# The second MoE layer takes its tokens in one chunk of 256 and four chunks of 512

## The chip, the cores and the metric

The kernel runs on one core of a Trainium2 chip. The metric is the device time of one execution in microseconds (us), as the median of several runs. Durations inside an execution come from one profiled execution, in which the engines are named PE (TensorE matmul), PEld (its weight load), DVE (VectorE), ACT (ScalarE), POOL (GpSimd) and SP (the engine that issues the transfers).

## What is computed

Attention with a decay mask makes 2304 token rows of 512 values. Two feed-forward layers (here "layer 1" and "layer 2", each 512 to 2048 to 512) follow:

```python
x = np.ascontiguousarray(attn_out.transpose(0, 2, 1, 3)).reshape(B * S, H * D)   # 2304 x 512
x = _moe_ref(x=x, **moe_kwargs)        # layer 1
return _moe2_ref(x=x, **moe2_kwargs)   # layer 2

def _moe2_ref(x, w_in, w_out):
    h = x @ w_in                                            # 512 -> 2048
    neg, pos = h <= -1.0, h >= 1.0
    g = np.where(pos, h, np.where(neg, 0.0, (h + 1.0) ** 2 / 4.0))
    return (g @ w_out).astype(np.float32)                   # 2048 -> 512
```

The weights arrive as 64-bit floats and are turned into pairs of fp32r tiles on the chip (a high and a low part). A product of two such pairs takes three matmuls: high by high, high by low, low by high.

## The kernel before

**Layer 2.** The tokens go in nine chunks of 256 (`C1`). The 2048 hidden values go in 16 slices of 128 (`NF`). For a chunk `c` and a slice `s`, `l2_slice` does this:

- `h` (L1052): the first product, 12 matmuls of 256 columns (four blocks of 128 input channels, three matmuls each) with the weight as the stationary operand, into one of two result banks `ps_h` (ring `h`, two slots).
- the activation on 128x256: `clip` on DVE (L1057), `square` on ACT (L1060), `both` on DVE (L1063), which is the last to read the bank; `ghi` on ACT (L1068) and `glo` on DVE (L1071) make the high and low part `gH`, `gL`. The result of the activation has four buffers (ring `g`), the pair `gH`, `gL` has three (ring `gg`).
- `y` (L1095): the second product, 3 matmuls of 512 columns for each group of 128 tokens, so two groups (`tg`) per slice, with `gH` or `gL` as the stationary operand and the weight streaming. Each group of tokens gathers over all 16 slices in a result bank `ps_z` of its own; two banks per chunk, in turn from `ps_a` and `ps_y`. After the last slice a copy (L1108) and a store (L1111) take it out.

In the text below a "first product" is such a block of 12 matmuls, a "group" is one block of 3 matmuls of the second product.

**The input of a chunk.** Layer 1 leaves its result in DRAM. `l2_x` loads 256 tokens of it (L1024, 512 KB) into one buffer `x2` and splits it into a high part (ACT, L1031) and a low part (DVE, L1034), four casts on each engine. The three input slots of layer 1 are used again.

**The weights of layer 2** come in 32 pieces. `convert` loads a piece (L831), and ACT and DVE turn it into the pair of fp32r tiles with seven instructions (ACT L840, L870; DVE L843, L849, L857, L862, L875; L862 is the last to read the loaded piece). This runs beside the end of layer 1 and the first chunk of layer 2.

**The order of the work.** The program is written by a list scheduler (`Order.emit`). Every task has an engine, a modelled duration and a place `pos`; the scheduler plays the engines against each other in modelled time, and takes on each engine, of the tasks whose inputs and buffers are ready in the model, the one with the lowest `pos`. What it writes is a fixed order for each engine. On the chip each engine keeps to that order and waits where an input or a buffer is not there.

Of the kernel before, what the change touches and what calls it, by code (L numbers as in the profile page):

```python
# [100 lines left out]
class Order:  # L101
# [91 lines left out]
def kernel(  # L193
# [33 lines left out]
    GLEAD = 4  # L227
# [29 lines left out]
    def pe(n, cnt=1):  # L257
        return cnt * (max(n, 240) / 2.4 + 13)
# [4 lines left out]
    def dve(n, ptr=False):  # L263
        return 68 + n * 1.042 + (60 if ptr else 0)
# [14 lines left out]
    for c in range(NC1):  # L279
# [16 lines left out]
    ps_a = l1.enter_context(tc.tile_pool(name="ps_a", bufs=1, space=PSUM))  # L296
    R = {n: Ring(k) for n, k in dict(
        raw=2, qr=1, qr1=1, q=2, k=2, S=7, M=3, r=2, PH=1, PL=1, s=3, o=1, h=2, g=4, gg=LH + 1,
        sums=2, rec=2, val1=1, raw2=NRAW, val2=NVAL, x2r=1, z0=1, z1=1).items()}

    for n in "soh":
        R[n].serial = True
# [143 lines left out]
    for u, pr in head_list():  # L446
# [135 lines left out]
        for j in range(2):  # L582
# [86 lines left out]
            for grp in groups:  # L669
# [333 lines left out]

    def open2():
        la.close()
        P2["p"] = l1.enter_context(tc.tile_pool(name="stage2", bufs=1, reuse_waits="tile"))

    t_open = add("X", 0, open2, -50, attn_tasks + conv1 + plain_pv)
    for i in range(NPIECE):
        convert(2, i, NF * NC1 + i / 2 + WOFF2, R["raw2"],  # L1010
                lambda b: P2["p"].tile([P, NCC, P], WT, tag=f"raw{b.slot}", name="raw"), [t_open], w_use[i])


    NTG = C1 // P
    PB = NF * NC1

    def l2_x(c):
        pos = PB + NF * (c - 1) + 4 if c else PB - 8
        rb = Buf(R["x2r"])
        i, o = divmod(c * C1, X2T)  # L1020

        def load():
            rb.t = P2["p"].tile([P, NCC, C1], F32, tag="x2", name="x2", bufs=1)
            nc.sync.dma_start(out=rb.t, in_=x2s[i][:, :, o:o + C1].rearrange("e p t -> p e t"))  # L1024

        ld = add("SP", 500, load, pos, [t_open] + x2_stores[c], new=[rb], move=moved(4 * P, 1024))
# [12 lines left out]
        return r

    def l2_slice(c, s, xr, prev_y, zb):
        pos = PB + NF * c + s
        hb, gb, gg = Buf(R["h"]), Buf(R["g"]), Buf(R["gg"])
# [11 lines left out]
        def clip():  # L1055
            gb.t = gp.tile([P, C1], F32, tag=f"g{gb.slot}", name="g")
            nc.vector.tensor_scalar(out=gb.t, in0=hb.t, scalar1=-1.0, scalar2=1.0, op0=ALU.max, op1=ALU.min)  # L1057

        def square():
            nc.scalar.activation(out=gb.t, in_=gb.t, func=AF.Square, scale=0.5, bias=half)  # L1060

        def both():
            nc.vector.tensor_tensor(out=gb.t, in0=hb.t, in1=gb.t, op=ALU.max)  # L1063

        def ghi():
            gg.t = (gp.tile([P, C1], F32R, tag=f"gH{gg.slot}", name="gH"),
                    gp.tile([P, C1], F32R, tag=f"gL{gg.slot}", name="gL"))
            nc.scalar.copy(out=gg.t[0], in_=gb.t)  # L1068

        def glo():  # L1070
            nc.vector.tensor_tensor(out=gg.t[1], in0=gb.t, in1=gg.t[0].bitcast(F32), op=ALU.subtract)  # L1071

        th = add("PE", pe(C1, 3 * NCC), h, pos - LH, xr + W_ready[2, 2 * s] + [last["h"]], new=[hb])
# [3 lines left out]
        a = last["g"] = add("DVE", dve(C1), clip, pg, [th, last["g"]], new=[gb], use=[hb])
        a = add("ACT", act(C1, True), square, pg, [a], use=[gb])
        a = add("DVE", dve(C1), both, pg, [a], use=[gb, hb])
        a = add("ACT", act(C1), ghi, pg, [a], new=[gg], use=[gb])  # L1080
        b = add("DVE", dve(C1), glo, pg, [a], use=[gb, gg])
        deps = [a, b] + prev_y + W_ready[2, 2 * s + 1]
        r = []
        for tg in range(NTG):
            def y(tg=tg):
                if s == 0:
                    if c % 2:
                        zb[tg].t = ps_y.tile([P, DM], F32, tag=f"y{tg}", name=f"ps_z{tg}")
                    else:
                        zb[tg].t = ps_a.tile([P, DM], F32, tag=f"{'so'[tg]}{zb[tg].slot}", name=f"ps_z{tg}")  # L1090
                wh, wl = W[2, 2 * s + 1]
                gh, gl = gg.t
                sl = slice(tg * P, (tg + 1) * P)
                for t, (a, b) in enumerate(((gh, wh), (gh, wl), (gl, wh))):
                    nc.tensor.matmul(out=zb[tg].t, lhsT=a[:, sl], rhs=b,  # L1095
                                     start=(s == 0 and t == 0), stop=(s == NF - 1 and t == 2))

            ty = add("PE", pe(DM, 3), y, pos, deps + zfree[c % 2][tg], new=[zb[tg]] if s == 0 else [],
                     use=[gg] + ([zb[tg]] if s else []))
            deps = [ty]  # L1100
            if s == NF - 1:
                ob = Buf(R["val2"])
                r0 = c * C1 + tg * P

                def ev(tg=tg, ob=ob):
                    ob.t = P2["p"].tile([P, DM], F32, tag=f"val{ob.slot}", name="osb")
                    eng = nc.vector.tensor_copy if tg % 2 else nc.scalar.copy
                    eng(out=ob.t, in_=zb[tg].t)  # L1108

                def st(ob=ob, r0=r0):  # L1110
                    nc.sync.dma_start(out=out[r0:r0 + P, :], in_=ob.t)  # L1111

                a = add("DVE" if tg % 2 else "ACT", dve(DM) if tg % 2 else act(DM), ev, pos - 1, [ty],
                        new=[ob], use=[zb[tg]])
                add("SP", 400, st, pos - 1, [a], use=[ob], move=moved(P, 2048))
        return [ty]

    zfree = {0: [[t_open]] * NTG, 1: [prev] * NTG}
    prev = []
    for c in range(NC1):  # L1120
        xr = l2_x(c)
        zb = [Buf(R["so"[tg]] if c % 2 == 0 else R[f"z{tg}"]) for tg in range(NTG)]
        for s in range(NF):
            prev = l2_slice(c, s, xr, prev, zb)

    order.emit()

# [29 lines left out]
```

## Time and profile before

| | us |
|---|---|
| median of 3 runs | 1093.48 (1092.68 to 1096.11) |
| the profiled execution | 1093.86 |
| its span, from the first to the last instruction | 1092.1 |
| TensorE busy in the span | 1028.2 (94%) |
| VectorE busy | 771.4 (71%) |
| ScalarE busy | 671.6 (61%) |

Layer 2 runs from 678.3 us of the span to the end. A timeline row reads: start in us, length in us, engine, line of the kernel, operation, the tile written and the tiles read, shape, count of instructions that the row joins, and in brackets the idle time before it with what ended that. Rows of PE overlap, since a matmul's length holds its way through the array; how far matmuls follow each other is read from the starts of rows. A row of the windows gives, for a stretch of the span, busy time and instructions of each engine, then the granted TensorE clock (1.00 is full speed), the busy share of the DMA engines and GB/s.

### The profile page before, as it was taken

What the parts mean: (1) busy time and instruction counts of PE and PEld (TensorE: products, weight loads), DVE (VectorE), ACT (ScalarE), POOL (GpSimd) and SP (SyncE); (2) the same over time, 40 slices, a digit from 0 to 9 for tenths busy, and PEclk for the clock granted to TensorE, in tenths of its full rate; (3) what the DMA queues carried; (4) which work ended last, traced back from release to release, by engine and by line L of the source; (5) the groups of instructions that cost most, each with busy time, mean ns of one, the idle gap of its engine ahead of it and who ended that gap; (6) DMA issues with size and microseconds to landing.
All of it is one profiled execution on the core that took longest, in us unless ns stands there. A gap on an engine that the chain in (4) does not pass through costs nothing.

```text
span 1092.1 us, 20791 instructions
## 1 busy us (share of the span) xinstructions
PE 1028.2 (94%) x7317; PEld 965.4 (88%) x7317; DVE 771.4 (71%) x1928; ACT 671.6 (61%) x1754; POOL 143.4 (13%) x244
## 2 busy tenths in 40 slices
PE   3569788999999999999998999999999999999998
PEld 2448588999999999999998999899999999999997
DVE  5999998778777787778765999965454544544443
ACT  5977868978888888988764476543333333333332
POOL 2422223222132212321110000000000000000000
PEclk9759989999999999999999999999999999999999
DMA  7555413312123121232104653410100001000000
GB/s 200 139 169 159 106 44 85 83 30 71 25 56 82 41 58 24 57 80 48 42 8 129 199 162 119 134 41 18 40 20 20 30 11 39 1 20 14 7 20 20
DMA packets 125656, 72.37 MB, mean 66 GB/s; under 512 B 89424, under 2 KB 119120, under 8 KB 125552
## 3 DMA queue, kind: packets, MB, share of 16 engines
q1 hardware_dynamic: 125552, 71.04, 23.9%
q8 instruction: 58, 0.95, 0.4%
q14 instruction: 46, 0.38, 0.1%
HBM read 61.42 MB, written 9.51 MB: 65 GB/s over the span
## 4 chain that ended last, share of the span: by engine, by line
PE 76%; DVE 7%; ACT 4%; issue 3%; POOL 1%; DMA 1%; SPq 0%; POOLq 0%; ACTq 0%; DVEq 0%
PE ps_h L1052 18%; PE ps_z L1095 18%; PE ps_y L961 15%; PE ps_h L922 15%; PE ps_s L605 3%; PE ps_o L714 1%; PE ps_o L722 1%; PE ps_o L720 1%; PE ps_o L721 1%; PE pst L531 1%; DVE w L875 1%; POOL Mb L661 1%; ACT S L680 1%; DVE kT L516 1%; PE pst L502 1%
## 5 line engine op out<-in xcount | busy, mean ns | idle before, releaser
L922 PE MATMUL ps_h<-x,w 128*128 128x256 f32 x1728 | 237.1, 287 | 6.2 <-DVE g L935 3.9
L1052 PEld LDWEIGHTS ps_h<-x,w 128*128 128x128 f32 x1728 | 226.0, 191 | 13.0 <-DVE g L1063 1.3
L961 PE MATMUL ps_y<-gH,w 128*128 128x256 f32 x1152 | 236.2, 288 | 0.0
L1052 PE MATMUL ps_h<-x,w 128*128 128x256 f32 x1728 | 229.9, 283 | 0.9 <-DVE g L1063 0.9
L922 PEld LDWEIGHTS ps_h<-x,w 128*128 128x128 f32 x1728 | 219.6, 192 | 8.8 <-DVE g L935 5.6
L961 PEld LDWEIGHTS ps_y<-gH,w 128*128 128x128 f32 x1152 | 190.4, 192 | 0.2 <-ACT gH L941 0.2
L1095 PE MATMUL ps_z<-w,gH 128*128 128x512 f32 x576 | 180.8, 395 | 0.0
L961 PE MATMUL ps_y<-gL,w 128*128 128x256 f32 x576 | 163.8, 284 | 0.9 <-DVE gL L944 0.8
L1060 ACT ACTIVATE g<-g,half 128x256 f32<-128x256 f32 x144 | 73.3, 509 | 128.7 <-DVE g L1057 128.6
L1071 DVE TENSOR_TENSOR gL<-g,gH 128x256 fp32r<-128x256 f32 x144 | 61.1, 425 | 96.3 <-ACT gH L1068 95.6
L1068 ACT CAST gH<-g 128x256 fp32r<-128x256 f32 x144 | 58.4, 406 | 109.7 <-PE ps_z L1095 106.7
L1063 DVE TENSOR_TENSOR g<-ps_h,g 128x256 f32<-128x256 f32 x144 | 61.0, 424 | 81.4 <-ACT g L1060 81.4
L961 PEld LDWEIGHTS ps_y<-gL,w 128*128 128x128 f32 x576 | 110.8, 192 | 1.8 <-DVE gL L944 1.8
L1095 PE MATMUL ps_z<-w,gL 128*128 128x512 f32 x288 | 112.0, 389 | 0.0
L618 ACT ACTIVATE S<-ps_s,nb 128x320 f32<-128x320 f32 (+3 forms) x224 | 100.1, 449 | 17.7 <-PE ps_s L605 15.7
L1095 PEld LDWEIGHTS ps_z<-w,gH 128*128 128x128 f32 x576 | 99.0, 190 | 12.7
L442 POOL TENSOR_SCALAR_AFFINE_SELECT S<-S 128x128 f32<-128x128 f32 (+1 forms) x160 | 62.6, 395 | 339.8 <-ACT S L618 330.7
L605 PE MATMUL ps_s<-qH,kT 128*128 128x320 f32 (+3 forms) x224 | 76.7, 343 | 16.5 <-ACT S L618 7.7
L935 DVE SCALAR_TENSOR_TENSOR g<-g,calpha,ps_h 128x256 f32<-128x256 f32 x144 | 68.7, 477 | 27.5 <-ACT g L932 26.5
L661 POOL PARTITION_ALL_REDUCE Mb<-Mx x64 | 78.9, 1233 | 65.1 <-ACT Mx L645 28.3
L680 ACT ACTIVATE S<-S 128x320 f32<-128x320 f32 (+1 forms) x192 | 79.2, 424 | 9.6 <-DVE S L677 8.8
L941 ACT CAST gH<-g 128x256 fp32r<-128x256 f32 x144 | 58.4, 405 | 38.4 <-DVE g L935 37.7
(81 smaller groups left out, 1600.8 us busy)
## 6 DMA issues: line engine op xcount, KB each, us to landing
raw<-in_moe_w_in_dram SPq DMA_DIRECT2D x32, 512.0 KB
raw<-in_moe_w_out_dram SPq DMA_DIRECT2D x32, 512.0 KB
x<-ysb SPq DMA_DIRECT2D x36, 128.0 KB
x<-x SPq DMA_DIRECT2D x9, 512.0 KB
out_dram<-osb SPq DMA_DIRECT2D x18, 256.0 KB
qr<-in_q_dram SPq DMA_DIRECT2D x64, 64.0 KB
raw<-in_k_dram SPq DMA_DIRECT2D x32, 128.0 KB
raw<-in_v_dram SPq DMA_DIRECT2D x24, 128.0 KB
```

The source lines that it names most:

```text
L442: nc.gpsimd.affine_select(out=sl, in_=sl, pattern=[[1, sl.shape[1]]], compare_op=ALU.is_ge, fill=NEG, base=base, channel_multiplier=-1)
L605: nc.tensor.matmul(out=sb.t[:, :m], lhsT=kt.t[:, kb * P:(kb + 1) * P], rhs=qt.t[t][:, qo:qo + m], start=(t == 0), stop=(t == 1))
L618: nc.scalar.activation(out=Sb.t[:, so:so + m], in_=sb.t[:, :m], func=AF.Identity, bias=bias)
L661: nc.gpsimd.partition_all_reduce(Mb.t[:, :n], Mx.t[:, :n], P, ReduceOp.max)
L680: ex = add("ACT", act(gn), lambda Sb=Sb, gn=gn: nc.scalar.activation(out=Sb.t[:, :gn], in_=Sb.t[:, :gn], func=AF.Exp, scale=-SCALE), pb_, ...
L922: nc.tensor.matmul(out=hb.t, lhsT=a[:, sl], rhs=b, start=(cc == 0 and t == 0), stop=(cc == NCC - 1 and t == 2))
L935: nc.vector.scalar_tensor_tensor(out=gb.t, in0=gb.t, scalar=calpha[:, s:s + 1], in1=hb.t, op0=ALU.mult, op1=ALU.add)
L961: nc.tensor.matmul(out=Y[c][e // 2][:, e % 2, :], lhsT=a[:, sl], rhs=b, start=(s == 0 and t == 0 and e % 2 == 0), stop=(s == NF - 1 and t ...
L1052: nc.tensor.matmul(out=hb.t, lhsT=a[:, sl], rhs=b, start=(cc == 0 and t == 0), stop=(cc == NCC - 1 and t == 2))
L1060: nc.scalar.activation(out=gb.t, in_=gb.t, func=AF.Square, scale=0.5, bias=half)
L1071: nc.vector.tensor_tensor(out=gg.t[1], in0=gb.t, in1=gg.t[0].bitcast(F32), op=ALU.subtract)
L1095: nc.tensor.matmul(out=zb[tg].t, lhsT=a[:, sl], rhs=b, start=(s == 0 and t == 0), stop=(s == NF - 1 and t == 2))
```

## The change

Layer 2 takes one chunk of 256 tokens and then four chunks of 512 (`wide2`). In a wide chunk:

- the first product has 12 matmuls of 512 columns instead of twice 12 of 256, and fills a whole bank `ps_h`; there are still two such banks;
- the activation still works on 128x256, so twice per slice, once for each half of the bank; a bank is free when both halves have been read;
- the second product has four groups of 3 matmuls per slice (here A, B, C, D; A and B read the first half's `gH`, `gL`, C and D the second half's). The four result banks come from a ring of six (`zz`);
- `g` keeps four buffers and `gH`, `gL` three, each for 256 tokens;
- the input is loaded in two halves of 256 tokens into two buffers (`x2w`) and split by eight casts on ACT and eight on DVE into one of two tiles `xw` of 512 tokens. These lie in a new pool, `stage3`, that takes the memory of `stage2`, the buffers of the weight conversion. It is opened after the conversion and the first chunk's input, in the order of the program; on the chip each new tile waits for the old tiles that it lies on.

```diff
-    def l2_x(c):
-        pos = PB + NF * (c - 1) + 4 if c else PB - 8
...
+    CW = 2 * C1
+    wide2 = [(0, 1)] + [(c, 2) for c in range(1, NC1, 2)]
...
+    def open3():
+        P2["x"].close()
+        P3["p"] = l1.enter_context(tc.tile_pool(name="stage3", bufs=1, reuse_waits="tile"))
+
+    R["xw"], R["x2w"], R["ox"], R["zz"] = Ring(2), Ring(2), Ring(4), Ring(6)
...
+    ZB = [(ps_y, "y0"), (ps_y, "y1"), (ps_a, "s0"), (ps_a, "s1"), (ps_a, "s2"), (ps_a, "o0")]
...
+    def l2_x(c, w, t_open3):
...
+        for hf in range(w):
+            rb = Buf(R["x2r"] if w == 1 else R["x2w"])
...
+                nc.sync.dma_start(out=rb.t, in_=x2s[i][:, :, o:o + C1].rearrange("e p t -> p e t"))
...
+    def l2_slice(c, w, s, xr, xb, prev_y, zb):
+        n = w * C1
+        pos = PB + NF * c + w * s
...
-            hb.t = ps_h.tile([P, C1], F32, tag=f"h{hb.slot}", name="ps_h")
+            hb.t = ps_h.tile([P, n], F32, tag=f"h{hb.slot}", name="ps_h")
...
-                xh, xl = X[NC1 + c][cc]
+                xh, xl = X[NC1 + c][cc] if w == 1 else (xb.t[:, cc, 0, :], xb.t[:, cc, 1, :])
...
+        for hf, (gb, gg) in enumerate(halves):
+            hs = slice(hf * C1, (hf + 1) * C1)
...
+                nc.vector.tensor_tensor(out=gb.t, in0=hb.t[:, hs], in1=gb.t, op=ALU.max)
...
+            for t2 in range(C1 // P):
+                tg = hf * (C1 // P) + t2
```

**In the middle of a chunk, PE.** In the kernel before, this is two slices of chunk 6; `ps_z0` and `ps_z1` are the result banks of its two groups of tokens, `w_...` the weight of a slice.

```order
L1095 MATMUL ps_z0_13090<-w_10728,gH_13377 128x512 x2
L1095 MATMUL ps_z0_13090<-w_10728,gL_13378 128x512
L1052 MATMUL ps_h_13435<-x_12436,w_10042 128x256 x12
L1095 MATMUL ps_z1_13117<-w_10728,gH_13377 128x512 x2
L1095 MATMUL ps_z1_13117<-w_10728,gL_13378 128x512
L1095 MATMUL ps_z0_13090<-w_10844,gH_13404 128x512 x2
L1095 MATMUL ps_z0_13090<-w_10844,gL_13405 128x512
L1052 MATMUL ps_h_13462<-x_12436,w_10113 128x256 x12
```

In the changed kernel, where one wide chunk ends and the next begins (in the middle of a chunk the blocks follow each other in the same way); `ps_z_11979`, `11983`, `11987` and `11995` are the banks of A, B, C and D of the old chunk.

```order
L1144 MATMUL ps_z_11987<-w_11034,gH_12583 128x512 x2
L1144 MATMUL ps_z_11987<-w_11034,gL_12584 128x512
L1097 MATMUL ps_h_12617<-xw_11761,w_10033 128x512 x12
L1144 MATMUL ps_z_11995<-w_11034,gH_12583 128x512 x2
L1144 MATMUL ps_z_11995<-w_11034,gL_12584 128x512
L1097 MATMUL ps_h_12644<-xw_11761,w_10061 128x512 x12
L1144 MATMUL ps_z_12668<-w_10083,gH_12595 128x512 x2
L1144 MATMUL ps_z_12668<-w_10083,gL_12596 128x512
L1144 MATMUL ps_z_12672<-w_10083,gH_12595 128x512 x2
L1144 MATMUL ps_z_12672<-w_10083,gL_12596 128x512
L1144 MATMUL ps_z_12676<-w_10083,gH_12611 128x512 x2
L1144 MATMUL ps_z_12676<-w_10083,gL_12612 128x512
```

Before, one group of second products stands on each side of the border between slices, and a first product in the middle of each slice. After, two first products come with only group D between them, then seven groups (A, B, C, D of one slice, A, B, C of the next), then again a first product, D, a first product. That is the pattern of two wide slices.

**In the middle of a chunk, ACT.** Before, in the same chunk 6 (L1068 is `ghi`, L1060 `square`):

```order
L1068 CAST gH_13431<-g_13331 128x256
L1060 ACTIVATE g_13448<-g_13448,half_99 128x256
L1068 CAST gH_13458<-g_13367 128x256
L1060 ACTIVATE g_13475<-g_13475,half_99 128x256
L1068 CAST gH_13485<-g_13394 128x256
```

After, in a wide chunk (L1122 is `ghi`, L1114 `square`):

```order
L1122 CAST gH_12845<-g_12770 128x256
L1122 CAST gH_12857<-g_12787 128x256
L1114 ACTIVATE g_12852<-g_12852,half_99 128x256
L1122 CAST gH_12871<-g_12808 128x256
L1114 ACTIVATE g_12869<-g_12869,half_99 128x256
L1114 ACTIVATE g_12890<-g_12890,half_99 128x256
L1122 CAST gH_12910<-g_12832 128x256
L1114 ACTIVATE g_12914<-g_12914,half_99 128x256
```

Casts and squares no longer alternate: a square can stand behind two casts, of which each waits for a group of second products to give back a `gH` buffer.

**From the first chunk to the second.** PE, changed kernel: `ps_z_10647` and `ps_z_10675` are the banks of the 256-token chunk, `xw_11090` is the input of the first wide chunk. Four more groups stand between this piece and the last first product of the 256-token chunk.

```order
L1144 MATMUL ps_z_10675<-w_10617,gH_11056 128x512 x2
L1144 MATMUL ps_z_10675<-w_10617,gL_11057 128x512
L1144 MATMUL ps_z_10647<-w_10714,gH_11083 128x512 x2
L1144 MATMUL ps_z_10647<-w_10714,gL_11084 128x512
L1144 MATMUL ps_z_10675<-w_10714,gH_11083 128x512 x2
L1144 MATMUL ps_z_10675<-w_10714,gL_11084 128x512
L1144 MATMUL ps_z_10647<-w_10835,gH_11105 128x512 x2
L1144 MATMUL ps_z_10647<-w_10835,gL_11106 128x512
L1097 MATMUL ps_h_11137<-xw_11090,w_9920 128x512 x12
L1144 MATMUL ps_z_10675<-w_10835,gH_11105 128x512 x2
```

SP, changed kernel, at the end of the weights' loads (L831) and with the first loads of wide chunks (L1053):

```order
L831 DMA raw_10845<-in_moe2_w_in_dram 128x4x128
L831 DMA raw_10881<-in_moe2_w_out_dram 128x512
L1053 DMA x2_11046<-x2_0_86 128x4x256
L1053 DMA x2_11050<-x2_0_86 128x4x256
L1053 DMA x2_11122<-x2_1_87 128x4x256
L1053 DMA x2_11150<-x2_1_87 128x4x256
```

ACT, changed kernel, at the same place (L1067 is the high part of the input):

```order
L1122 CAST gH_11056<-g_10960 128x256
L1114 ACTIVATE g_11077<-g_11077,half_99 128x256
L1122 CAST gH_11083<-g_10992 128x256
L1067 CAST xw_11090<-x2_11046 128x256 x4
L1122 CAST gH_11105<-g_11032 128x256
L1067 CAST xw_11090<-x2_11050 128x256 x4
```

Before, the second and the third chunk's input were loaded among the weights, and the chunk's first products began under the first chunk's second products. Now the wide chunk's input is loaded behind the last weight, and eight groups stand between the last narrow and the first wide first product.

## Rows read from the trace of the kernel before

**Rows 1.** The page: busy us of each engine.

```profile
PE 1028.2 (94%) x7317; PEld 965.4 (88%) x7317; DVE 771.4 (71%) x1928; ACT 671.6 (61%) x1754; POOL 143.4 (13%) x244
```

**Rows 2.** Windows: the end of the weight conversion, and the rest of layer 2.

```profile
600.00:716.00 116.00, 115.13 (x909) 112.34 (x908) 115.19 (x261) 70.14 (x153) 0.00 (x0) 1.00 0.48 146
716.00:1088.00 372.00, 372.00 (x2360) 337.33 (x2359) 179.44 (x426) 131.64 (x296) 0.00 (x0) 1.00 0.06 21
```

**Rows 3.** Groups by line, from 678 us on: busy us, mean ns, idle before.

```profile
L1052 PE MATMUL ps_h<-x,w 128*128 128x256 f32 x1728 | 229.9, 283 | 0.9 <-DVE g L1063 0.9
...
L1095 PE MATMUL ps_z<-w,gH 128*128 128x512 f32 x576 | 180.8, 395 | 0.0
L1095 PE MATMUL ps_z<-w,gL 128*128 128x512 f32 x288 | 112.0, 389 | 0.0
```

**Rows 4.** The chain that ended last: start us, us, what.

```profile
735.48 1.43 PE ps_h L1052 x12
...
1076.70 1.43 PE ps_h L1052 x12
```

**Rows 5.** Timeline of PE, the last first product and the groups behind it.

```profile
1076.54 1.59 PE L1052 MATMUL ps_h<-x,w 128*128 128x256 f32 x12
1077.97 0.63 PE L1095 MATMUL ps_z<-w,gH 128*128 128x512 f32 x2
...
1078.67 0.62 PE L1095 MATMUL ps_z<-w,gH 128*128 128x512 f32 x2
...
1079.36 0.62 PE L1095 MATMUL ps_z<-w,gH 128*128 128x512 f32 x2
...
1087.52 0.62 PE L1095 MATMUL ps_z<-w,gH 128*128 128x512 f32 x2
```

**Rows 6.** Timeline of PE: layer 2's first blocks, and its one stall.

```profile
678.30 1.60 PE L1052 MATMUL ps_h<-x,w 128*128 128x256 f32 x12
...
681.18 1.60 PE L1052 MATMUL ps_h<-x,w 128*128 128x256 f32 x12
...
684.06 0.63 PE L1095 MATMUL ps_z<-w,gH 128*128 128x512 f32 x2
...
690.72 1.69 PE L1052 MATMUL ps_h<-x,w 128*128 128x256 f32 x12 [0.85 <-DVE g L1063]
```

**Rows 7.** Timeline of DVE at that stall.

```profile
690.25 0.75 DVE L1063 TENSOR_TENSOR g<-ps_h,g 128x256 f32<-128x256 f32 x2
```

**Rows 8.** Timeline of DVE: the end of the weight conversion.

```profile
713.57 0.68 DVE L862 SCALAR_TENSOR_TENSOR val<-raw,val 128x512 int32<-128x512 int32 x1
...
715.17 0.68 DVE L875 TENSOR_TENSOR w<-val,w 128x512 fp32r<-128x512 f32 x1
```

**Rows 9.** Timeline of SP: the last weight load, and two loads of input.

```profile
701.91 0.33 SPq L831 DMA_DIRECT2D raw<-in_moe_w_out_dram  x1
716.58 7.33 SPq L1024 DMA_DIRECT2D x<-x  x2
```

**Rows 10.** Windows of 1 us behind the load at 716.58.

```profile
719.00:720.00 1.00, 1.00 (x10) 1.00 (x9) 0.41 (x1) 0.00 (x0) 0.00 (x0) 1.00 0.74 252
720.00:721.00 1.00, 1.00 (x8) 0.87 (x7) 0.05 (x1) 0.48 (x2) 0.00 (x0) 1.00 0.00 0
```

**Rows 11.** Timeline of ACT: casts of an input, then a cast and a square.

```profile
720.83 1.02 ACT L1031 CAST x<-x 128x256 fp32r<-128x256 f32 x3
...
1080.01 0.41 ACT L1068 CAST gH<-g 128x256 fp32r<-128x256 f32 x1 [0.97 <-PE ps_z L1095]
1080.33 0.51 ACT L1060 ACTIVATE g<-g,half 128x256 f32<-128x256 f32 x1
```

**Rows 12.** Timeline of DVE behind these two, and the last copy.

```profile
1080.45 0.43 DVE L1071 TENSOR_TENSOR gL<-g,gH 128x256 fp32r<-128x256 f32 x1 [0.49 <-ACT gH L1068]
1080.86 0.42 DVE L1063 TENSOR_TENSOR g<-ps_h,g 128x256 f32<-128x256 f32 x1
...
1088.40 0.69 DVE L1108 COPY osb<-ps_z 128x512 f32<-128x512 f32 x1 [3.44 <-PE ps_z L1095]
```

More of the change, by code (lines that the diff above doesn't have):

```diff
@@ new lines, with load, hi, lo @@
+    ZB = [(ps_y, "y0"), (ps_y, "y1"), (ps_a, "s0"), (ps_a, "s1"), (ps_a, "s2"), (ps_a, "o0")]
+    for x in range(6):
+        b0_ = Buf(R["zz"])
+        b0_.users = list(prev) if x < 2 else [t_open]
+        R["zz"].slots[x] = b0_
+    def l2_x(c, w, t_open3):
+        if w == 1:
+            rb = Buf(R["x2r"])
+            pos = PB - 8
+        else:
+            pos = PB + NF * (c - 1) + 4
+        i, o = divmod(c * C1, X2T)
+        xb = Buf(R["xw"])
+        r = []
+        for hf in range(w):
+            rb = Buf(R["x2r"] if w == 1 else R["x2w"])
+            i, o = divmod((c + hf) * C1, X2T)
+            def load(rb=rb, i=i, o=o):
+                rb.t = (P2["p"].tile([P, NCC, C1], F32, tag="x2", name="x2", bufs=1) if w == 1 else
+                        P3["p"].tile([P, NCC, C1], F32, tag=f"x2{rb.slot}", name="x2"))
+                nc.sync.dma_start(out=rb.t, in_=x2s[i][:, :, o:o + C1].rearrange("e p t -> p e t"))
+            ld = add("SP", 500, load, pos, [t_open if w == 1 else t_open3] + x2_stores[c + hf], new=[rb],
+                     move=moved(4 * P, 1024))
+            if w == 1:
+                free2.append(ld)
+            for cc in range(NCC):
+                def hi(cc=cc, rb=rb, hf=hf):
+                    if w == 1:
+                        x = xt(NC1 + c)[cc][0]
+                    else:
+                        if xb.t is None:
+                            xb.t = P3["p"].tile([P, NCC, 2, CW], F32R, tag=f"xw{xb.slot}", name="xw")
+                        x = xb.t[:, cc, 0, hf * C1:(hf + 1) * C1]
+                    nc.scalar.copy(out=x, in_=rb.t[:, cc, :])
+                def lo(cc=cc, rb=rb, hf=hf):
+                    if w == 1:
+                        xh, xl = xt(NC1 + c)[cc]
+                    else:
+                        xh, xl = (xb.t[:, cc, z, hf * C1:(hf + 1) * C1] for z in range(2))
+                    nc.vector.tensor_tensor(out=xl, in0=rb.t[:, cc, :], in1=xh.bitcast(F32), op=ALU.subtract)
+                first_ = w == 2 and hf == 0 and cc == 0
+                a = add("ACT", act(C1), hi, pos + cc, [ld] + (h1_tasks[NC1 - RC] if w == 1 else r[:1]),
+                        new=[xb] if first_ else [], use=[rb] + ([] if w == 1 or first_ else [xb]))
+                r += [a, add("DVE", dve(C1), lo, pos + cc, [a], use=[rb] + ([xb] if w == 2 else []))]
+                if w == 1:
+                    free2.extend(r[-2:])
+        return r, xb
@@ L1053, in h @@
                                      start=(cc == 0 and t == 0), stop=(cc == NCC - 1 and t == 2))
[L1055 to L1073, printed above, removed]
+        th = add("PE", pe(n, 3 * NCC), h, pos - (LH if w == 1 else 3), xr + W_ready[2, 2 * s] + [last["h"]],
+                 new=[hb], use=[xb] if w == 2 else [])
@@ L1074, in l2_slice @@
         last["h"] = th
-        h1_tasks.setdefault(NC1 + c, []).append(th)
         pg = pos - GLEAD
[L1077 to L1115, printed above, removed]
@@ L1116, in l2_slice, with clip, square, both @@
-        return [ty]
-    zfree = {0: [[t_open]] * NTG, 1: [prev] * NTG}
-    prev = []
-    for c in range(NC1):
-        xr = l2_x(c)
-        zb = [Buf(R["so"[tg]] if c % 2 == 0 else R[f"z{tg}"]) for tg in range(NTG)]
+        r = prev_y
+        for hf, (gb, gg) in enumerate(halves):
+            hs = slice(hf * C1, (hf + 1) * C1)
+            def clip(gb=gb, hs=hs):
+                gb.t = gp.tile([P, C1], F32, tag=f"g{gb.slot}", name="g")
+                nc.vector.tensor_scalar(out=gb.t, in0=hb.t[:, hs], scalar1=-1.0, scalar2=1.0, op0=ALU.max,
+                                        op1=ALU.min)
+            def square(gb=gb):
+                nc.scalar.activation(out=gb.t, in_=gb.t, func=AF.Square, scale=0.5, bias=half)
+            def both(gb=gb, hs=hs):
+                nc.vector.tensor_tensor(out=gb.t, in0=hb.t[:, hs], in1=gb.t, op=ALU.max)
+            def ghi(gb=gb, gg=gg):
+                gg.t = (gp.tile([P, C1], F32R, tag=f"gH{gg.slot}", name="gH"),
+                        gp.tile([P, C1], F32R, tag=f"gL{gg.slot}", name="gL"))
+                nc.scalar.copy(out=gg.t[0], in_=gb.t)
+            def glo(gb=gb, gg=gg):
+                nc.vector.tensor_tensor(out=gg.t[1], in0=gb.t, in1=gg.t[0].bitcast(F32), op=ALU.subtract)
+            a = last["g"] = add("DVE", dve(C1), clip, pg + hf, [th, last["g"]], new=[gb], use=[hb])
+            a = add("ACT", act(C1, True), square, pg + hf, [a], use=[gb])
+            a = add("DVE", dve(C1), both, pg + hf, [a], use=[gb, hb])
+            a = add("ACT", act(C1), ghi, pg + hf, [a], new=[gg], use=[gb])
+            b = add("DVE", dve(C1), glo, pg + hf, [a], use=[gb, gg])
+            deps = [a, b] + W_ready[2, 2 * s + 1]
+            for t2 in range(C1 // P):
+                tg = hf * (C1 // P) + t2
+                def y(tg=tg, t2=t2, gg=gg):
+                    if s == 0:
+                        pool, tag = ZB[zb[tg].slot]
+                        zb[tg].t = pool.tile([P, DM], F32, tag=tag, name="ps_z")
+                    wh, wl = W[2, 2 * s + 1]
+                    gh, gl = gg.t
+                    sl = slice(t2 * P, (t2 + 1) * P)
+                    for t, (a, b) in enumerate(((gh, wh), (gh, wl), (gl, wh))):
+                        nc.tensor.matmul(out=zb[tg].t, lhsT=a[:, sl], rhs=b,
+                                         start=(s == 0 and t == 0), stop=(s == NF - 1 and t == 2))
+                ty = add("PE", pe(DM, 3), y, pos, deps + r, new=[zb[tg]] if s == 0 else [],
+                         use=[gg] + ([zb[tg]] if s else []))
+                r = [ty]
+                if s == NF - 1:
+                    ob = Buf(R["ox"])
+                    r0 = c * C1 + tg * P
+                    def ev(tg=tg, ob=ob):
+                        pool = xp if ob.slot < 2 else P3["p"]
+                        ob.t = pool.tile([P, DM], F32, tag=f"x{ob.slot + 1}" if ob.slot < 2 else f"o{ob.slot}",
+                                         name="osb")
+                        eng = nc.vector.tensor_copy if tg % 2 else nc.scalar.copy
+                        eng(out=ob.t, in_=zb[tg].t)
+                    def st(ob=ob, r0=r0):
+                        nc.sync.dma_start(out=out[r0:r0 + P, :], in_=ob.t)
+                    a = add("DVE" if tg % 2 else "ACT", dve(DM) if tg % 2 else act(DM), ev, pos - 1, [ty],
+                            new=[ob], use=[zb[tg]])
+                    add("SP", 400, st, pos - 1, [a], use=[ob], move=moved(P, 2048))
@@ L1123 @@
+        return r
+    free2 = list(conv2)
+    t_open3 = None
+    prev = []
+    for c, w in wide2:
+        if w == 2 and t_open3 is None:
+            t_open3 = add("X", 0, open3, -50, free2)
+            for x in (2, 3):
+                b0_ = Buf(R["ox"])
+                b0_.users = [t_open3]
+                R["ox"].slots[x] = b0_
+        xr, xb = l2_x(c, w, t_open3)
+        zb = [Buf(R["zz"]) for _ in range(w * C1 // P)]
         for s in range(NF):
-            prev = l2_slice(c, s, xr, prev, zb)
+            prev = l2_slice(c, w, s, xr, xb, prev, zb)
```

32 lines of the change are left out of this document (10 added, 22 removed).

## The prediction

> **What bounds the kernel now.** I read the page first: PE is busy 94% of the span [rows 1], but such a share mixes stages, so the windows come next. From 716 us, when the weights are converted, PE is busy 372.00 of 372.00 us at a granted clock of 1.00 (2.4 GHz), while DVE works 179 us and ACT 132 us [rows 2]. Up to 716 us DVE is the full engine (115.2 of 116 us), and PE still works 115.1 us. The groups by line say the same from the other side: in all of layer 2, PE stands idle 0.9 us ahead of first products and 0.0 ahead of second ones [rows 3]. The chain that ended last shows the beat: from 735.48 to 1076.70 us there are 122 first products, 121 steps in 341.22 us, 2.82 us for each slice of 256 tokens [rows 4], also across the borders of chunks. So layer 2 is a row of matmuls without a gap, and only a change of what the matmuls themselves take, or a new gap, can move the time.
>
> **What a matmul costs, by its width.** The timeline's starts give it [rows 5]. A first product (12 x 256 columns) holds PE from 1076.54 to 1077.97, 1.43 us, or 0.119 for each matmul. Behind the last first product groups follow groups: from 1079.36 to 1087.52 there are twelve, 8.16 us, 0.68 each, 0.2267 for each matmul of 512 columns. The group right behind a first product takes 0.70 (1077.97 to 1078.67), the one ahead of the next 0.69 (1.43 + 0.70 + 0.69 is the 2.82). Twice 0.119 is 0.238, so each matmul has a fixed part of 0.012 us, which a 512-wide one pays once.
>
> **The sum for the wide chunks.** Removed: in eight chunks, 16 slices each, 12 of every 24 first-product matmuls, 768 in all. No trace of before has a first product of 512 columns. The nearest row is the second product: the same width, the same fp32r operands, a new weight for each matmul, the same kind of bank. I take its 0.2267, so 12 make 2.72 us. From above the bound is twice the narrow one, 2.86; from below I know of no row that shows 512 columns faster, so 2.72 is the lower end too. The pattern of two wide slices is then two first products (5.44), D between them (0.71, a seam on both sides), A behind a first product (0.70), five plain groups (3.40), C ahead of a first product (0.69): 10.94 us. Before, the same work was four beats of 2.82: 11.28. That is 0.34 for two wide slices, and there are 32 such pairs: **10.9 us** less. About 9 of them are the fixed parts (64 x 0.14), the rest seams.
>
> The Trainium skill has a rule that speaks against this: "TensorE: Matmul & The Clock Gate", section "Back-to-back issue gap", gives N/2.4 ns plus 2.5 ns for a warm matmul, so 109.2 ns for 256 columns and 215.8 for 512. By that, the 768 matmuls would save 1.9 us, and the time would be 1091.6. The trace does not agree with the size: its matmuls stand 119 and 227 ns apart.
>
> **What is unchanged.** The activation keeps its count and its shapes, DVE and ACT stay near half load behind 716 us. Loads (nine) and stores (18) are the same. The last piece is the same too: group D of the last slice, a copy by DVE (1088.40, 0.69 us [rows 12]), a store. The first chunk still runs 16 beats of 2.82.
>
> **The bank of a first product.** Two banks remain, and each is now read by two activations, one behind the other. Where it is tightest is the bank that a first product takes over ahead of D. Follow its last half: it has no `g` buffer until the cast and `glo` of an older slice have freed one, and that cast waits for a group B to give back `gH`. Count from the end of that B. Cast to `glo` 0.44 (1080.01 to 1080.45 [rows 11, 12]); `clip` right behind it, at about 0.8; but the square stands behind the second cast, which waits for group D, two groups later: 1.36. Cast to square 0.32, square to `both` 0.53 (1080.33 to 1080.86 [rows 11, 12]), `both` to PE 0.47 (690.25 to 690.72 [rows 6, 7]). In sum 2.68 us. PE meanwhile does C, D, A, B, C, 3.4 us. So 0.7 us is left, and I cost the wait at nothing; its cover is those five groups. How little that cover is makes it a rival below.
>
> **From the narrow to the wide chunk.** The input of the first wide chunk can't be loaded among the weights any more. Is it late? When the first group starts, at 684.06, two of the narrow chunk's first products are done (678.30 and 681.18) [rows 6]. By the order, the other 14 and 19 groups come before the last of them ends: 14 x 1.43 + 19 x 0.69, and the old stall of 0.85, lead to 718.0. Eight groups then follow, so the first wide product is due at 723.5. The first load stands right behind the last weight load (701.91 before [rows 9]). The second needs a released buffer; at the latest that is the last reading of a loaded weight, 713.57 + 0.68 [rows 8]. A load is over 3.4 us after its issue (716.58, the DMA engines quiet from 720.0 [rows 9, 10]), so it is there by 717.7. ACT's casts stand behind a cast that waits for the first of the eight groups, 718.7; nine more pieces of 0.31 (three take 1.02, of which the last is 0.40 [rows 11]) end at 721.8, DVE's low parts reach PE 0.9 later, 722.7. That is 0.8 us early for the last block of channels, more for the first. The next wide chunk's loads start as these casts free the buffers, at 721.2 and 722.8, and land by 726.2, when the first wide product ends; its bank is not needed before 730. So no wait there either, by a margin of about 1 us.
>
> DVE has seven input casts fewer to do before the last conversion (they came from the second and third chunk), some 2.3 us, so PE's stall of 0.85 (for `both` behind conversions, [rows 6, 7]) may shrink or move; its ends are a gain of 0.85 and a loss of about as much. I take zero.
>
> **The sum.** Span 1092.1 - 10.9 = 1081.2; with the 1.76 us around it (1093.86 - 1092.1) 1083.0 for a run like the profiled one. That run lay 0.38 above the median, so the median after is **1082.6 us**.
>
> **Rivals.**
> - **The input comes late** (faster, but less). If both loads wait for the last conversion (715.17 + 0.7 [rows 8]) and the second, as in the trace, is issued some 7 us behind the first (7.33 for both, less one issue [rows 9]), it lands at 726.3; the casts reach PE 1.8 us later, 728.1, against 723.5: 4.6 us lost, 1087.2. For it: the new pool lies on the conversion's buffers. Against it: there are two buffers now, and the second load of before waited for casts, not for memory.
> - **The bank comes late** (slower). If the square had to wait for one cast more, two groups later, the chain would be 4.04 us against 3.4: 0.64 for each pair, 32 times 20.5 us, 1103.1. From 3.74 on (3.4 + 0.34) the gain is gone. For it: two halves, one bank, a square behind two casts. Against it: 0.7 us of room, and no step of the chain is taken from a better place than it will have.
> - **The fixed part doesn't go** (no change). If a 512-wide first product took twice the narrow one, 2.86, a pair would take 11.22, and 32 x 0.06 = 1.9 us be won: 1091.6. That would be so if the 0.012 us lay with the streamed columns and not with the matmul. The 0.2267 of the second product speaks against it. The rule of the Trainium skill named above gives the same time by another road.
>
> **How the numbers follow.** My forecast has a chance of 0.85, with a range of its own of 1080.5 to 1084.5 (the stall gone, or one more of 1 to 2 us). The late input has 0.07, the late bank 0.04, the fixed part 0.04. No change here means within 0.3%, 3.3 us. Faster: 0.85 + 0.07 = 0.92; same 0.04; slower 0.04. The range goes from 1080.0 to 1087.5: it takes in the late input and leaves the last two out.
>
> **What would show it.** In the profile after: first products of 512 columns x768 and of 256 x192; starts of wide first products and their next group 2.72 us apart; a pair of wide slices in 10.94 us; idle time of PE ahead of first products near 1 us in all. Wrong would be: steps of 2.86 (the fixed part); idle time before every second first product, ended by `both` on DVE (the bank); one long idle time near 720 us ended by the casts of the input (the load).

## The result, and the profile after

| us | before | after |
|---|---|---|
| median | 1094.18 (4 runs) | 1082.40 (4 runs, 1079.94 to 1083.87) |
| the profiled execution | 1093.86 | 1081.37 |
| its span | 1092.1 | 1079.6 |

The ratio is 0.9889, with a 95% interval of 0.9863 to 0.9916; the forecast's own ratio, 1082.6 to 1093.48, is 0.9900. Here before was run beside after, so its median isn't quite the one shown ahead.

The page of the changed kernel, as in [rows 1]:

```profile
PE 1015.3 (94%) x6549; PEld 925.0 (86%) x6549; DVE 764.9 (71%) x1928; ACT 665.7 (62%) x1754; POOL 143.5 (13%) x244
```

PE has 768 matmuls fewer, and DVE and ACT have as many instructions as before. The windows, as in [rows 2]:

```profile
600.00:716.00 116.00, 115.59 (x915) 112.98 (x914) 113.05 (x251) 67.47 (x146) 0.00 (x0) 1.00 0.49 149
716.00:1075.00 359.00, 359.00 (x1591) 297.54 (x1591) 174.35 (x434) 128.94 (x303) 0.00 (x0) 1.00 0.06 20
```

PE is again busy throughout from 716 us to 1075, at the full clock: no gap came in there, and what was won is time of matmuls. The chain that ended last (start, us, what; 21 matmuls are seven groups, 51 are 17), to be laid beside [rows 4]:

```profile
763.02 4.76 PE ps_z L1144 x21
767.78 2.72 PE ps_h L1097 x12
771.18 2.72 PE ps_h L1097 x12
773.90 4.76 PE ps_z L1144 x21
...
1064.26 11.57 PE ps_z L1144 x51
```

From 763.02 to 773.90 is a pair of wide slices: 10.88 us, 48 matmuls at 0.2267. The beat repeats to the end. In PE's timeline one sees that the width of the tile makes no difference any more:

```profile
900.90 0.61 PE L1144 MATMUL ps_z<-w,gH 128*128 128x512 f32 x2
...
901.58 2.88 PE L1097 MATMUL ps_h<-xw,w 128*128 128x512 f32 x12
904.30 0.62 PE L1144 MATMUL ps_z<-w,gH 128*128 128x512 f32 x2
...
904.98 0.62 PE L1144 MATMUL ps_z<-w,gH 128*128 128x512 f32 x2
...
909.06 2.88 PE L1097 MATMUL ps_h<-xw,w 128*128 128x512 f32 x12
...
912.46 2.88 PE L1097 MATMUL ps_h<-xw,w 128*128 128x512 f32 x12
```

Group D ahead of a wide product (900.90 to 901.58) and group A behind it (904.30 to 904.98) take 0.68 each, as a group among groups does. Before they took 0.69 and 0.70 [rows 5].

**Layer 2 apart from the rest.** From the first of its products to the end of its last group, before takes from 678.30 [rows 6] to 1088.37 (by the chain, whose last piece begins at 1078.13 and takes 10.24): 410.07 us. After takes from 676.09 to 1064.26 + 11.57 = 1075.83: 399.74 us. In both a few blocks of layer 1, 1.44 us each, still stand among the first of these, two before (from 679.74 and 682.62) and four after (from 677.53, 680.41, 683.29 and 685.42); without them it is 407.19 and 393.98, 13.2 us less. The profiled executions are 12.5 us apart: the part ahead took 0.7 us longer after.

### The profile page after: what moved, and what is told of

Read it like the earlier page. It is cut to its first block, busy times and chain, and to the rows that moved or that the text cites. A ratio compares the mean times of both kernels' runs of the same rounds, so it can differ in the third digit from the quotient of the medians.

```text
span 1079.6 us, 19362 instructions
## 1 busy us (share of the span) xinstructions
PE 1015.3 (94%) x6549; PEld 925.0 (86%) x6549; DVE 764.9 (71%) x1928; ACT 665.7 (62%) x1754; POOL 143.5 (13%) x244
## 4 chain that ended last, share of the span: by engine, by line
PE 76%; issue 8%; DVE 7%; ACT 5%; POOL 2%; DMA 2%; SPq 0%; POOLq 0%; ACTq 0%; DVEq 0%
PE ps_h L1097 18%; PE ps_z L1144 18%; PE ps_y L961 15%; PE ps_h L922 15%; PE ps_s L605 3%; PE ps_o L714 1%; PE ps_o L722 1%; PE ps_o L720 1%; PE ps_o L721 1%; POOL Mb L661 1%; PE pst L531 1%; DVE S L677 1%; ACT S L680 1%; POOL S L442 1%; DVE kT L516 1%
## 5 line engine op out<-in xcount | busy, mean ns | idle before, releaser
L922 PE MATMUL ps_h<-x,w 128*128 128x256 f32 x1728 | 236.8, 287 | 6.3 <-DVE g L935 5.3
L922 PEld LDWEIGHTS ps_h<-x,w 128*128 128x128 f32 x1728 | 219.4, 192 | 8.8 <-DVE g L935 6.7
L1097 PE MATMUL ps_h<-xw,w 128*128 128x512 f32 x768 | 184.5, 389 | 0.0
L1144 PE MATMUL ps_z<-w,gH 128*128 128x512 f32 x576 | 177.7, 390 | 0.0
L1097 PEld LDWEIGHTS ps_h<-xw,w 128*128 128x128 f32 x768 | 144.2, 188 | 29.9
L1122 ACT CAST gH<-g 128x256 fp32r<-128x256 f32 x144 | 58.6, 407 | 161.4 <-PE ps_z L1144 160.7
L1144 PEld LDWEIGHTS ps_z<-w,gH 128*128 128x128 f32 x576 | 107.2, 188 | 21.3
L1114 ACT ACTIVATE g<-g,half 128x256 f32<-128x256 f32 x144 | 73.3, 509 | 70.0 <-DVE g L1110 69.8
L1117 DVE TENSOR_TENSOR g<-ps_h,g 128x256 f32<-128x256 f32 x144 | 60.9, 423 | 39.9 <-ACT g L1114 39.3
L932 ACT ACTIVATE g<-ps_h 128x256 f32<-128x256 f32 x144 | 54.9, 381 | 43.6 <-PE ps_h L922 42.7
```

What stands on the lines that cost most here:

```text
L922: nc.tensor.matmul(out=hb.t, lhsT=a[:, sl], rhs=b, start=(cc == 0 and t == 0), stop=(cc == NCC - 1 and t == 2))
L1097: nc.tensor.matmul(out=hb.t, lhsT=a[:, sl], rhs=b, start=(cc == 0 and t == 0), stop=(cc == NCC - 1 and t == 2))
L1144: nc.tensor.matmul(out=zb[tg].t, lhsT=a[:, sl], rhs=b, start=(s == 0 and t == 0), stop=(s == NF - 1 and t == 2))
```

## The experiments

The theory is that of the prediction: each matmul has a fixed part which a 512-wide one pays once, and the bank and the input have cover. The rivals are that something else in the new arrangement (its order, its banks, its buffers) gave the gain, that the floor lies elsewhere than in a fixed part, and that a cover is not what it was said to be. Every kernel is the changed one with one edit. In the cuts of code below, `...` stands for what is left out.

**The changed kernel again**, unedited.

> The changed kernel as it is, for a closer interval beside the others of this group. Theory (the gain is the fixed part of 768 matmuls and the seams between blocks of different width): a pair of wide slices takes 10.88 us, so 32 x 0.40 = 12.8 us less in layer 2, ratio 0.988 to 0.990. Rival (the first figure was a lucky draw and the forecast's 10.9 us is the truth): ratio 0.990 to 0.991.

1080.94 us (5 runs), ratio 0.9888 (0.9865 to 0.9911): the same once more, but the interval holds both expectations, so only the trace can choose between them. Its profiled execution had a span of 1083.8, 4.2 us more than that of after, and yet its layer 2 runs from 680.34 to 1080.09, 399.75 us against 399.74. What differs between these two executions lies ahead of layer 2; a trace tells far smaller differences in layer 2 than the total can.

**Two matmuls of 256 for each of 512**, into the same bank; all else stays.

```diff
-  nc.tensor.matmul(out=hb.t, lhsT=a[:, sl], rhs=b, ...
+  for k, (p0, p1) in enumerate([(0, 256), (256, 512)] if w == 2 else [(0, C1)]):
+      nc.tensor.matmul(out=hb.t[:, p0:p1], lhsT=a[:, sl], rhs=b[:, p0:p1], ...
```

> Each 512-wide matmul of the first product is issued as two of 256 columns into the two halves of the same bank; chunks, banks, loads, casts and the order of all blocks stay those of the changed kernel. Theory: 24 matmuls of 256 columns at 0.12 us make 2.88 instead of 2.72, and the seams come back (four per pair of slices, 0.01 to 0.02 each), so a pair takes about 11.25 us, 32 x 0.37 = 12 us more: the time of the kernel before, 1092 to 1096. Rival (the gain comes from the new order, the loads or the banks): it stays near 1082.

1091.75 us (12 runs), ratio 0.9979 (0.9967 to 0.9991). Of its trace, first the chain, then PE's timeline:

```profile
752.75 4.79 PE ps_z L1146 x21
...
763.98 4.79 PE ps_z L1146 x21
```

```profile
895.67 3.03 PE L1098 MATMUL ps_h<-xw,w 128*128 128x256 f32 x24
898.54 0.63 PE L1146 MATMUL ps_z<-w,gH 128*128 128x512 f32 x2
...
899.23 0.63 PE L1146 MATMUL ps_z<-w,gH 128*128 128x512 f32 x2
```

The pair takes 11.23 us, 24 matmuls 2.87 (0.1196 each), the group behind them 0.69. Layer 2 runs from 675.53 to 1086.36, 410.83 us, 11.1 more than with matmuls of 512. So the width of the matmuls carries 11.1 of the 13.2 us, with the new order, banks and buffers in place in both. The rest comes with the arrangement: without its four blocks of layer 1, layer 2 takes 405.07 us here, 2.1 less than before, near the sum of two parts: 11.23 in place of 11.28 per pair, as the widths meet half as often (32 x 0.05 = 1.6 us), and a smaller stall early in layer 2 (0.4 us, below). (The medians are 2.4 us apart, by an interval of 1.0 to 3.6.)

**Four matmuls of 128**, in the same loop, with `[(0, 128), (128, 256), (256, 384), (384, 512)]`.

> As before, but each matmul of the first product in four of 128 columns. Theory (a fixed part of 0.0133 us for each matmul, whatever its width): 48 x (0.0533 + 0.0133) = 3.20 us for a first product, a pair 6.40 + 5.44 + seams = 11.9, 32 x 1.0 = 33 us more than the changed kernel, about 1115. Rival (the fixed part goes with the columns): 1094, like two of 256. Second rival (a weight load can't follow another in 0.067 us): clearly more than 1115.

1251.56 us, ratio 1.1441 (1.1417 to 1.1465). PE's timeline:

```profile
902.32 5.47 PE L1098 MATMUL ps_h<-xw,w 128*128 128x128 f32 x48
907.63 0.69 PE L1146 MATMUL ps_z<-w,gH 128*128 128x512 f32 x2
```

48 matmuls take 5.31 us, 0.1106 each. With 512 columns at 0.2267 and 256 at 0.1196, 256 columns cost 0.1071 and the fixed part is 0.0125; that alone would give 0.066 here. So with 128 columns something else holds: in this stream a matmul takes 0.11 us, and each has a weight load of its own (3072 loads for 3072 matmuls), as the second rival said. The loads speak for that rival: in the stream they start 0.108 to 0.112 us apart and each matmul 0.058 to 0.061 behind its load, while between matmuls of 512 columns a load starts 0.003 behind the matmul before it. It is not shown by itself, as no run has narrow matmuls without loads. 2 x (5.31 - 2.72) x 32 = 166 us is nearly the whole loss. The kernel before, at 0.1196, stood 0.009 above this floor.

**384 and 128 columns**, in the same loop, with `[(0, 384), (384, 512)]`: as many matmuls as with twice 256.

> Each 512-wide matmul of the first product is issued as one of 384 and one of 128 columns. In the run with four of 128 a matmul of 128 columns took 0.111 us where a fixed part of 0.0133 would make 0.067. Theory A (a matmul costs its columns and a fixed part of 0.0133): 0.173 + 0.067 = 0.24, as two of 256: 1091 to 1093. Theory B (a matmul with a weight of its own never takes less than about 0.111, since the next weight is loaded behind it; 256 columns with 0.12 are hardly above that): 0.187 + 0.111 = 0.298, 12 make 3.57 instead of 2.72, 64 x 0.85 = 54 us more than the changed kernel, about 1136.

1129.10 us, ratio 1.0316 (1.0296 to 1.0336). PE's timeline:

```profile
901.47 3.54 PE L1098 MATMUL ps_h<-xw,w 128*128 128x384 f32 x24
904.85 0.68 PE L1146 MATMUL ps_z<-w,gH 128*128 128x512 f32 x2
```

24 matmuls take 3.38 us. A fixed part alone would leave the 2.87 of twice 256. With the floor, 0.1106 for 128 columns and 0.173 for 384 (midway between 0.1196 and 0.2267) give 12 x 0.284 = 3.40. So theory B has the better of it; its 1136 was 7 us too much, as it took 0.187 for 384 columns and no seams. A wide neighbour doesn't make up for a narrow one. Only the sum of the two is read here: single starts stand 0.23 us behind a matmul of 384 columns and 0.06 behind one of 128, and they don't say to which of the two the time belongs.

**Half of the change**: five chunks of 256, then two of 512 (the input and output buffers of the narrow chunks as in the kernel before).

```diff
-    wide2 = [(0, 1)] + [(c, 2) for c in range(1, NC1, 2)]
+    wide2 = [(c, 1) for c in range(5)] + [(c, 2) for c in range(5, NC1, 2)]
```

> Half of the change: chunks 0 to 4 of 256 tokens, then two of 512. The input of the second to fifth chunk is loaded and cast as in the kernel before. Theory: 16 pairs at 0.40 instead of 32, so half the gain, 6.4 us, 1087 to 1089. Rival (the gain comes at the first chunk's border, where the loads moved): as much as the full change or nothing.

1087.81 us, ratio 0.9945 (0.9927 to 0.9963), about half of the gain. In its trace layer 2, without two blocks of layer 1, takes 400.76 us, 6.4 less than before. The gain goes with the number of wide slices, and the early part of the change (input, pool, first border) has little to do with it: this kernel has the old stall of 0.85 us.

**One copy more per activation**: ACT makes a copy of 128x256, which nobody reads, ahead of each square of a wide chunk.

```diff
             def square(gb=gb):
+                for _ in range(1 if w == 2 else 0):
...
+                    nc.scalar.copy(out=P3["idle"], in_=gb.t)
```

> The changed kernel with one copy of 128x256 on ACT (0.31 us, into a tile that nobody reads) ahead of every square of a wide chunk. It lengthens what must happen before a bank of first products is free. Theory (the bank has 0.7 us to spare for the first product ahead of D, about 1.1 us for the one behind D, whose chain holds two squares): 0.31 and 0.62 us more fit in, the time stays within 0.3% of the changed kernel, 1079 to 1085, and no first product waits. Rival (the banks are on the edge, or ACT's time counts): 0.3 us or more in each of 32 pairs, 1092 or more.

1083.61 us, ratio 0.9895 (0.9876 to 0.9913), not to be told from the changed kernel. But the room is used up. DVE's timeline has the last `both` of the bank that the product behind D takes, PEld's the weight loads of that product, PE's the product:

```profile
913.91 0.42 DVE L1121 TENSOR_TENSOR g<-ps_h,g 128x256 f32<-128x256 f32 x1 [1.01 <-ACT g L1118]
```

```profile
914.45 2.59 PEld L1097 LDWEIGHTS ps_h<-xw,w 128*128 128x128 f32 x12 [0.17 <-issue]
```

```profile
914.55 2.92 PE L1097 MATMUL ps_h<-xw,w 128*128 128x512 f32 x12
```

It is the first weight load that waits for the bank: a waiting instruction of PE's load queue stands 0.46 us behind the start of `both`, and the load 0.08 behind that. In the changed kernel the load starts 0.22 us ahead of its product, right behind the start of the matmul before. Here it starts 0.13 later than that, and the product behind D takes 2.75 us in place of 2.72. For the product ahead of D the load is just in time. The pairs take 10.92 us in place of 10.88, 1.1 us over all 32 (layer 2 as a whole is 2.1 longer, 401.80 us), too little for the median to show. So the expectation had the time right and the sizes wrong: a copy takes 0.41 us and not 0.31, and behind D three of them come in and not two, as the next run shows.

**Two copies more**, the same edit with `range(2 ...)`.

> Two such copies ahead of every square. Theory: the chain behind D holds two squares, so 1.24 us more against 1.1 to spare: 0.1 to 0.6 us of waiting in each pair, 5 to 18 us more than the changed kernel, 1086 to 1100; the waits stand at first products behind D and are ended by the last reading of the bank on DVE. Rival (the room is larger than read): no change.

1124.73 us, ratio 1.0277 (1.0255 to 1.0299): the side was right, the size far too small. The chain over one pair of wide slices shows why (L1126 is `ghi`, L1117 the copies, L1118 the square, L1121 `both`, L1110 `clip`):

```profile
755.12 3.00 PE ps_h L1097 x12
...
760.65 0.41 ACT gH L1126
761.06 0.32 ACT idle L1117
...
761.84 0.52 ACT g L1118
...
762.72 0.42 DVE g L1110
...
764.04 0.52 ACT g L1118
...
765.01 0.34 DVE g L1110
...
766.25 0.52 ACT g L1118
766.79 0.44 DVE g L1121
...
767.36 0.70 PE ps_h L1097 x2
```

The pair takes 12.24 us (755.12 to 767.36), 1.36 more than 10.88; 32 pairs make 43.5, and the median is 42.3 above that of after. From the cast at 760.65 to PE at 767.36 three activations stand one behind the other: the copies and the square of the next wait for its `clip`, and that stands behind the last one's `both` in DVE's order. Six copies of 0.42 are in this chain, not four of 0.31 as the expectation had it. Taken from it, they leave 12.24 - 2.55 = 9.7 us, so without copies the ring of PE, ACT and DVE has about 1.2 us per pair to spare (worked out, for this chain), and with three copies, one for each activation, it comes to 10.96: hardly over the 10.88 that PE needs. With one copy the pair took 10.92 (906.55 to 917.47 in that chain). Not only the product behind D is late here: the one ahead of D starts at 762.95, 0.23 us behind the end of its groups, and each of the two takes 2.80 to 2.85 us.

**A late input**: the second half of the first wide chunk's input is loaded six times in a row into its buffer.

```diff
-                nc.sync.dma_start(out=rb.t, ...
+                for _ in range(6 if late else 1):
+                    nc.sync.dma_start(out=rb.t, ...
```

> The second half of the first wide chunk's input is loaded six times, one load behind the other, so that it lands 5 x 3.2 = 16 us later, at about 730 instead of 714. Theory (it was there 9.6 us before the first wide product began, at 724.1): 9.6 of the 16 us are hidden and PE waits once for 6 to 8 us, ended by the casts of the input, 1088 to 1090. Rival (the input was already what PE waited for): all 16 us come on top, 1097 or more.

1093.57 us, ratio 0.9992 (0.9979 to 1.0005): the whole gain is gone, 3.6 to 5.6 us more than expected. The rows for it are ACT's and PE's timeline, then windows of 5 us:

```profile
735.12 1.32 ACT L1068 CAST xw<-x 128x256 fp32r<-128x256 f32 x4 [11.90 <-DMA x<-x]
```

```profile
735.58 4.54 PE L1098 MATMUL ps_h<-xw,w 128*128 128x512 f32 x12 [9.79 <-ACT xw L1068]
739.96 0.62 PE L1145 MATMUL ps_z<-w,gH 128*128 128x512 f32 x2
```

```profile
730.00:735.00 5.00, 0.00 (x0) 0.00 (x0) 0.00 (x0) 0.00 (x0) 0.00 (x0) 0.50 0.59 185
735.00:740.00 5.00, 4.42 (x13) 3.45 (x14) 2.11 (x6) 2.55 (x8) 0.00 (x0) 0.62 0.43 139
740.00:745.00 5.00, 5.00 (x24) 4.12 (x23) 4.84 (x15) 3.58 (x10) 0.00 (x0) 1.00 0.03 11
```

The five added loads end at 735, later than thought, and PE stands idle 9.79 us. That is not all: while it is idle the granted clock falls to 0.50 (1.2 of 2.4 GHz), and the first wide product behind it takes 4.38 us (735.58 to 739.96) in place of 2.72. 9.79 + 1.66 = 11.45; the median is 11.2 above that of after. This wait thus cost more than its length.

## Why the prediction was right, and which term was off

**The matmuls, right; the term of the seams, mis-sized.** The step "12 make 2.72 us" held to the hundredth: from the first start of a wide product to the start of the block behind it, all 64 take 2.72. The 768 matmuls are alike in length too:

```profile
L1097 PE MATMUL ps_h<-xw,w x768: 388/389/390, 724.1 to 1063.9; 128*128 128x512 f32 x192
...
L1097 PE MATMUL ps_h<-x,w x192: 277/283/385, 676.1 to 718.5; 128*128 128x256 f32 x192
```

(This is the line's view: count, shortest, median and longest matmul in ns with its way through the array, first and last start.) The pair was forecast at 10.94 and took 10.88. The forecast gave D 0.71, A 0.70 and C 0.69, that is 0.06 of seams, as if they belonged to the border between a first and a second product. They belong to the border between two widths: between blocks of 512 there are none, with matmuls of 256 in the same places there are 0.05 per pair. So a pair gives 0.40 in place of 0.34, 32 pairs 12.8 us in place of 10.9: 9.6 from the fixed parts (64 x 0.15, from 2.87 - 2.72) and 3.2 from the seams.

**The stall, left at zero, gave 0.4 us.** PE's timeline, for [rows 6]:

```profile
693.74 1.70 PE L1097 MATMUL ps_h<-x,w 128*128 128x256 f32 x12 [0.41 <-DVE g L1117]
```

The 0.85 us became 0.41, a gain inside the 0.85 that the prediction named as an end. The kernel with half of the change, whose early inputs are cast as before, keeps the 0.85; that fits the prediction's reason, seven casts fewer on DVE, which was not tried by itself. 12.8 + 0.4 are the 13.2 us by which layer 2 became shorter.

**Why 1082.6 came out so close all the same.** 1.9 us of seams and 0.4 of the stall were not counted; the profiled execution took back 0.7 ahead of layer 2; and the medians of 4 runs each are uncertain by some 3 us (0.9863 to 0.9916 of 1094). That the median came within 0.2 us of the forecast is luck; the trace settles the terms, the median alone would not.

**The fixed part doesn't go** fell: steps of 2.72, not 2.86. By the rule of the Trainium skill ("TensorE: Matmul & The Clock Gate", section "Back-to-back issue gap", N/2.4 plus 2.5 ns) 256 and 512 columns would take 109.2 and 215.8 ns, and 128 columns 55.8. The section gives this formula for an isolated matmul, and says that in a stream with weight loads it counts too little at small N and too much at large N. The runs show 119.6, 226.7 and 110.6: too little at all three widths of these fp32r matmuls, so at 128 columns the trace agrees with the section and at 512 it does not.

**The bank** caused no wait, as forecast, and the chain came as worked out; its room was measured to the wrong end. ACT's and DVE's timeline behind the group B that ends at 905.66:

```profile
905.63 0.41 ACT L1122 CAST gH<-g 128x256 fp32r<-128x256 f32 x1 [2.15 <-PE ps_z L1144]
906.99 0.41 ACT L1122 CAST gH<-g 128x256 fp32r<-128x256 f32 x1 [0.95 <-PE ps_z L1144]
907.31 0.51 ACT L1114 ACTIVATE g<-g,half 128x256 f32<-128x256 f32 x1
```

```profile
906.07 0.42 DVE L1125 TENSOR_TENSOR gL<-g,gH 128x256 fp32r<-128x256 f32 x1 [2.13 <-ACT gH L1122]
906.53 0.42 DVE L1110 TENSOR_SCALAR g<-ps_h 128x256 f32<-128x256 f32 x1
907.43 0.43 DVE L1125 TENSOR_TENSOR gL<-g,gH 128x256 fp32r<-128x256 f32 x1 [0.48 <-ACT gH L1122]
907.85 0.42 DVE L1117 TENSOR_TENSOR g<-ps_h,g 128x256 f32<-128x256 f32 x1
...
910.91 0.42 DVE L1117 TENSOR_TENSOR g<-ps_h,g 128x256 f32<-128x256 f32 x1 [0.64 <-ACT g L1114]
```

The first cast starts as B ends, `glo` 0.44 later, `clip` at 0.9, the second cast at 1.36, the square 0.32 behind it, `both` at 907.85. With 0.47 to PE that is 908.32, and the next first product begins at 909.06: 0.74 us to spare, forecast 0.7. The bank of the next product, behind group D, has its last `both` at 910.91; with 0.47 that is 911.38, and PE takes it at 912.46, 1.1 us to spare. These rows stand at the border of two chunks, with the output's copies among them; in the middle of a chunk the second is 1.4 (`both` at 965.03, the product at 966.86). But what waits is the weight load, 0.22 us ahead of its product and 0.08 behind the waiting instruction (the run with one copy). To the load the room is 0.3 us less: 0.45 ahead of D, and behind D 0.8 at a border and 1.1 in the middle. The 0.47, read at a stall [rows 6, 7], had hidden that. The prediction followed only the first of the two. With copies the second gives way first, since three activations in a row lead to it; its 1.1 us is near the 1.2 worked out from two copies.

**The input** was there. PE's and ACT's timeline, and that of SP:

```profile
718.63 0.63 PE L1144 MATMUL ps_z<-w,gH 128*128 128x512 f32 x2
...
724.10 2.88 PE L1097 MATMUL ps_h<-xw,w 128*128 128x512 f32 x12
```

```profile
720.06 1.32 ACT L1067 CAST xw<-x 128x256 fp32r<-128x256 f32 x4
...
721.60 1.32 ACT L1067 CAST xw<-x 128x256 fp32r<-128x256 f32 x4
...
725.77 0.71 ACT L1067 CAST xw<-x 128x256 fp32r<-128x256 f32 x2 [1.97 <-DMA x<-x]
```

```profile
702.04 0.33 SPq L831 DMA_DIRECT2D raw<-in_moe_w_out_dram  x1
702.42 30.08 SPq L1053 DMA_DIRECT2D x<-x  x6
```

The last narrow product ends at 718.63 (forecast 718.0), the first wide one begins at 724.10 (723.5), straight behind the eight groups. The load had more room than forecast: in windows of 1 us the DMA engines carry 146 GB/s from 713 to 714 and nothing from there to 717, so its second half was there by 714 (717.7 at the latest in the forecast), and ACT turned to it at 721.60. The casts had less: they end at 722.9, against 721.8, as they began only at 720.06, and DVE's low parts end at 723.7, 0.4 us ahead of the product where the prediction had 0.8. The next wide chunk's casts wait for their load until 725.77 (by 726.2 at the latest in the forecast), and PE doesn't feel it. So the rival "the input comes late" did not occur.

**What stays open.** What the fixed part of 0.0125 us is, no run shows; the runs show that it goes with the number of matmuls at 256 and 512 columns. Whether the 0.11 us at 128 columns is the weight load's or the matmul's own was not tried. Nor was it tried to widen the first products of layer 1, whose inputs do not lie side by side.

## What to carry to other kernels

Where PE is busy without a gap and its matmuls each load a weight, count matmuls as well as columns: divide the starts in the timeline by the count for each width that the trace has, and a width that is missing can be priced from the other product of the same kernel. Price a seam by the two blocks that meet there, not by the roles that they play. Measure the room of a bank to the weight load that waits for it, not to the matmul behind it. When other engines do the same work in larger portions, follow every buffer around its ring, since an instruction that is added to each turn can stand in the chain three times.

## What was not expected of the hardware

- In streams of one width, each with a weight load of its own, a matmul takes 0.1106 us with 128 columns, 0.1196 with 256 and 0.2267 with 512 (fp32r, full clock): from 256 to 128 columns almost nothing is saved.
- Blocks of 512 columns join without loss. A group of 512-wide matmuls behind 256-wide ones takes 0.69 to 0.70 us in place of 0.68, behind 128-wide ones 0.76 (907.63 to 908.39 in the kernel with four of 128).
- In 9.79 us without a matmul the granted clock fell to 0.50, and the product behind it lost 1.66 us more.
- The first weight load of a block waits for the result bank: 0.13 us late, it made the 12 matmuls behind it 0.03 us longer (one copy).
- Layer 2 took 399.74 and 399.75 us in two executions whose spans were 4.2 us apart.
